# One store of a fused scan and adapter kernel, issued as 16 transfers of 8 partitions

## The chip, the core and the metric

The kernel runs on one core of a Trainium2 chip. The metric is the time of one execution on the device in microseconds (us). A measurement of this kernel repeats within about 0.2%.

## What is computed

The first part is a linear recurrence along 6400 steps for 8 sequences of 128 channels; the second adds, for each of the 51200 resulting rows, the weighted output of two of eight low-rank adapters.

```python
h = np.zeros((B, D))                       # B, S, D = 8, 6400, 128
for t in range(S):
    h = a[:, t] * h + b[:, t]
    out[:, t] = h
x = out.reshape(B * S, D)                  # 51200 x 128
topk = the two largest of x @ w_gate       # w_gate: 128 x 8
w = softmax over these two
x + sum over the two of w * ((x @ A[e]) @ B[e])   # A: 8 x 128 x 16, B: 8 x 16 x 128
```

The inputs a and b are 26.2 MB each, the output is 26.2 MB, all in float32.

## The kernel before

The 51200 rows are cut into 100 units of 512 rows (`UT`). For each unit w or v:

- `AB`: TensorE transposes a and b of the unit (64-row blocks, line 88) into `pA` and `pB`, so that the channels lie on partitions; ScalarE copies a to `a_st` (`aev`).
- `scan`: one VectorE scan instruction over 512 steps makes x in `xT`, in float16, from the last value of the unit before.
- `L`, the gating steps and `sig`: logits, the two largest, a sigmoid, in groups of units.
- `Z`, `mul`, `T`, `tev`: x times all adapters' A, times the gates, transposed back.
- `R` and `D`: x and the adapters' outputs are summed in `pO`; `oev` copies `pO` to a slot of `outt`, which holds `NOUT` = 24 units. In the last ten units (`TAIL`) VectorE may do this copy too; before that it is ScalarE's.
- `st`: a store of two units (one at either end: units 0, 1 and 96 to 99) from `outt` to the output. With two units a partition holds 1024 numbers, 4 KB, which are contiguous in the output; a store of two units is 128 such rows, 512 KB. Loads have the same shape.

Nothing is ordered by hand. `_Plan` (from line 94) takes every operation with its cost, its key (unit plus an offset by kind) and what it depends on, simulates the engines, and writes out one instruction list for each engine, with waits on semaphores in between. All loads and stores are issued by SP on one queue, in the planner's order, by `add_dma` (line 303), which gives each slot of `outt` a semaphore of its own that a transfer raises by 16. The lines concerned:

- `store(j)`, line 841: a store of units from u0 on has the key u0 + `HOLD` (24), and while u0 + 24 is under `FREE` (96) it also waits for the scan of unit u0 + 24. So stores run 24 units behind the scan, and the store of units 60 and 61 waits for the scan of unit 84. It is the first store after the last load on SP.
- `o_evac(v)`, line 819: the copy of unit v waits for the store that frees its slot, that of unit v - 24. So the copies of units 84 and 85 wait for the store of units 60 and 61.
- `ends`, line 875: SP's last instruction waits for the last 24 stores.

After the last load come 22 stores: 18 of two units and four of one.

Of the kernel before, what the change touches and what calls it, by code (L numbers as in the profile page):

```python
# [23 lines left out]
HOLD = 24  # L24
FREE = 96
# [7 lines left out]
NOUT = 24  # L33
TAIL = 10
FILLS = 1


class _Op:
# [55 lines left out]
class _Plan:  # L94
# [9 lines left out]
    def add(self, name, eng, kind, unit, cost, emit, deps=(), dma=None, bank=None, mode=None):  # L104

        engs = (eng,) if isinstance(eng, str) else eng
        cost = cost if isinstance(cost, dict) else {e: cost for e in engs}
        self.ops[name] = _Op(name, engs, kind, unit, cost, emit, list(deps), dma, bank, mode)
# [98 lines left out]
def bass_associative_scan_2x2__then__mixture_of_adapters_kernel(  # L207
# [8 lines left out]
    NB, S, D = a.shape  # L216
# [34 lines left out]
    with ExitStack() as stack:  # L251
# [20 lines left out]
        outt = sb(nc.sbuf_tensor("outt", [128, NOUT, UT], F32))  # L272
# [30 lines left out]
        def add_dma(name, eng, unit, starts, slot, time, deps=()):  # L303

            if slot not in dma_sem:
                dma_sem[slot] = [sb(nc.semaphore("q_" + "_".join(map(str, slot)))), 0]
            dma_sem[slot][1] += 16 * len(starts)
            sem, value = dma_sem[slot]

            def emit(h):  # L310
                for dst, src in starts:
                    last = h.dma_start(dst, src).then_inc(sem, 16)
                return last

            add(name, eng, "dma", unit, (450.0 * len(starts), 0.0), emit, deps, (sem, value, time))
# [54 lines left out]
        def fill(w):  # L370


            def emit(h):
                for _ in range(3):
                    last = h.matmul(pO[1][:, :], warm_t[:, 0:128], warm_t[:, :])
                return last

            add(f"fill{w}", "pe", "fix", 1000.0, (600.0, 800.0), emit, [f"AB{w}"])

        for w in range(FILLS):  # L380
            fill(w)
# [410 lines left out]
        def delta(v):  # L792
            def emit(what):
                def run(h):
                    for q, w in [(q, w) for q in range(Q) for w in what]:
                        left, right = {"x": (x_rows(v, q), ident_h[:, :]), "d": (zw_rows(v, q), Bcat_h)}[w]
                        last = h.matmul(
                            pO[v % NO][:, q * 128 : (q + 1) * 128],
                            left,
                            right,  # L800
                            start=w == "x" and q == 0,
                            stop=w == "d",
                            skip_group_check=True,
                        )
                    return last

                return run
# [7 lines left out]
            else:  # L815
                add(f"R{v}", "pe", "R", v, (223.0, 423.0), emit("x"), deps, mode="full")
                add(f"D{v}", "pe", "D", v, (220.0, 420.0), emit("d"), [f"R{v}", "cstB"] + tevs, mode="full")

        def o_evac(v):
            def emit(h):  # L820
                copy = h.tensor_copy if plan.ops[f"oev{v}"].eng == "dve" else h.copy
                return copy(outt[:, v % NOUT, :], pO[v % NO][:, :])  # L822

            tail = v >= NU - TAIL
            add(
                f"oev{v}",
                ("act", "dve") if tail else "act",
                "oev",
                v,
                {"act": (477.0, 645.0), "dve": (600.0, 745.0)} if tail else (477.0, 645.0),  # L830
                emit,
                [f"D{v}", f"st{store_of.get(v - NOUT)}"],
            )

        stores, u = [], 0
# [3 lines left out]
        store_of = {v: j for j, (u0, n) in enumerate(stores) for v in range(u0, u0 + n)}  # L839

        def store(j):
            u0, n = stores[j]
            s0 = u0 % NOUT
            rows = out[u0 * UT : (u0 + n) * UT, :].rearrange("(p i) d -> p (i d)", p=128)
            add_dma(
                f"st{j}",
                "sp",
                u0 + HOLD,
                [(rows, outt[:, s0 : s0 + n, :].rearrange("p n c -> p (n c)"))],
                ("o", s0, n),  # L850
                1.036 * ((625.0 if n == 2 else 650.0) * n + 13.0),
                [f"oev{v}" for v in range(u0, u0 + n)] + [f"scan{u0 + HOLD}"] * (u0 + HOLD < FREE),
            )

        for w in range(NU):
            for t in "ab":
# [6 lines left out]
        for v in range(NU):  # L863
            logits(v)
            z_mm(v)
            z_mul(v)
            zw_tr(v)
            t_evac(v)
            delta(v)
            o_evac(v)  # L870
        for k in range(len(groups)):
            gating(k)
        for j in range(len(stores)):
            store(j)
        ends = [f"st{j}" for j in range(len(stores) - NOUT, len(stores))]
        add("end", "sp", "fix", 1.0e9, (10.0, 10.0), lambda h: h.nop(), ends)

        plan.schedule(700.0, 3000.0, lambda t: 400.0, 94.0)
# [49 lines left out]
```

## Time and profile before

| | |
|---|---|
| median of 3 runs | 204.37 us (204.33 to 204.53) |
| the profiled execution | 204.59 us, span 202.5 us |
| TensorE / VectorE / ScalarE / GpSimd busy | 191.3 / 183.6 / 175.4 / 115.5 us |
| moved by DMA | 79.35 MB, 392 GB/s in the mean |
| TensorE's granted clock | 0.994 |

The span is that of the profiled instructions and transfers on the core; the execution's own time contains a start and an end beside it. Busy times overlap each other, so they say which engines are near their limit and not what ends last. A DMA share is the mean busy share of the core's 16 DMA engines: 1.0 is all sixteen at work, 1/16 (0.06) is one of them. "To landing" is from the issue of a transfer on SP to the last of the 16 steps by which its semaphore rises, and so tells of its slowest engine. L312 is the line of the `dma_start` call in `add_dma`.

### The profile page before, as it was taken

The numbers are of one execution on the slowest core, as the hardware profiler recorded it, in microseconds if no ns is written. First come the engines' busy times: TensorE is split into PE (matmuls) and PEld (weight loads), VectorE is DVE, ScalarE is ACT, GpSimd is POOL, SyncE is SP. The second block draws the span as 40 slices with busy tenths as digits, with TensorE's granted clock in tenths as the row PEclk, the third lists the DMA queues.
The fourth block names the chain that finished last, engine by engine and source line by source line (L and its number), as shares of the span: only waits on it lengthen the run. The fifth ranks groups of instructions, "written<-read, shape, count | busy, mean of one in ns | idle before, by whom it ended". The sixth has DMA issues, their size and how long they took to land.

```text
span 202.5 us, 8755 instructions
## 1 busy us (share of the span) xinstructions
PE 191.3 (94%) x3594; PEld 171.2 (85%) x3594; DVE 183.6 (91%) x272; ACT 175.4 (87%) x385; POOL 115.5 (57%) x234
## 2 busy tenths in 40 slices
PE   7888898999999999999999999999999999999990
PEld 3667777889899999999999999999999999999880
DVE  1599889999999999999999999999999999989960
ACT  2357977788999999999999999999999999989981
POOL 1326775766656746746665674675666575874300
PEclk9999999999999999999999999999999999999997
DMA  7999999999999999999999999999999999997875
GB/s 177 401 410 409 403 408 405 405 404 408 410 408 412 412 414 414 408 413 413 410 411 416 414 411 412 413 412 415 410 415 410 411 413 416 409 414 313 317 302 198
DMA packets 23687, 79.35 MB, mean 392 GB/s; under 512 B 3680, under 2 KB 3808, under 8 KB 23648
## 3 DMA queue, kind: packets, MB, share of 16 engines
q1 hardware_dynamic: 22320, 78.65, 97.2%
q8 instruction: 29, 0.48, 1.0%
q10 hardware_dynamic: 1328, 0.14, 0.5%
q14 instruction: 10, 0.08, 0.1%
HBM read 52.56 MB, written 26.21 MB: 389 GB/s over the span
## 4 chain that ended last, share of the span: by engine, by line
PE 83%; ACT 6%; DVE 4%; issue 3%; POOL 2%; DVEq 0%
PE pA L88 27%; PE pO L84 23%; PE pTL L88 14%; PE pZ L84 10%; PE pTL L84 5%; DVE xT L511 3%; PE pB L88 3%; ACT a_st L492 3%; PE pB L84 2%; ACT outt L822 1%; ACT zwT L787 1%; ACT z_sb L716 1%; DVE mx L590 1%; POOL zw L730 1%; ACT Lg L584 0%
## 5 line engine op out<-in xcount | busy, mean ns | idle before, releaser
L511 DVE TENSOR_TENSOR_SCAN xT<-a_st,xT,pB 128x512 f16<-128x512 f32 x96 | 120.2, 1252 | 3.8 <-ACT a_st L492 1.3
L492 ACT COPY a_st<-pA 128x512 f32<-128x512 f32 x100 | 60.7, 607 | 19.1 <-PE pB L88 14.9
L88 PE MATMUL pA<-ident_f,a_in 64*128 64x64 f32 (+1 forms) x792 | 71.8, 230 | 2.8 <-ACT a_st L492 1.9
L88 PE MATMUL pB<-ident_f,b_in 64*128 64x64 f32 (+1 forms) x792 | 71.7, 230 | 0.3 <-issue 0.2
L88 PEld LDWEIGHTS pA<-ident_f,a_in 64*128 64x128 f32 (+1 forms) x792 | 57.8, 139 | 11.3 <-ACT a_st L492 3.3
L822 ACT COPY outt<-pO 128x512 f32<-128x512 f32 x97 | 60.0, 626 | 0.7 <-PE pO L84 0.2
L787 ACT COPY zwT<-pTL 128x512 f16<-128x512 f16 x95 | 58.5, 615 | 0.4 <-PE pTL L88 0.3
L88 PEld LDWEIGHTS pB<-ident_f,b_in 64*128 64x128 f32 (+1 forms) x792 | 57.4, 138 | 1.1 <-issue 0.8
L730 DVE TENSOR_TENSOR zw<-pZ,g 128x512 f16<-128x512 f32 x76 | 51.5, 680 | 1.4 <-PE pTL L88 0.8
L84 PE MATMUL pO<-ident_h,xT 128*128 128x128 f16 x400 | 41.5, 228 | 0.2
L84 PE MATMUL pZ<-cst_h,xT 128*128 128x128 f16 x400 | 38.1, 219 | 0.0
L84 PE MATMUL pO<-cst_h,zwT 128*128 128x128 f16 x400 | 37.3, 218 | 0.8 <-ACT zwT L787 0.4
L88 PE MATMUL pTL<-ident_h,zw 128*128 128x128 f16 x380 | 37.7, 222 | 0.0
L730 POOL TENSOR_TENSOR zw<-z_sb,g 128x512 f16<-128x512 f32 x24 | 25.4, 1060 | 20.1 <-PE pTL L84 18.3
L84 PEld LDWEIGHTS pO<-ident_h,xT 128*128 128x128 f16 x400 | 32.8, 147 | 0.8 <-ACT outt L822 0.3
L84 PE MATMUL pTL<-cst_h,xT 128*128 128x8 f16 x400 | 27.5, 174 | 1.0 <-DVE xT L511 0.9
L84 PEld LDWEIGHTS pZ<-cst_h,xT 128*128 128x128 f16 x400 | 27.8, 114 | 0.1
L88 PEld LDWEIGHTS pTL<-ident_h,zw 128*128 128x128 f16 x380 | 21.6, 97 | 6.0
L84 PEld LDWEIGHTS pO<-cst_h,zwT 128*128 128x128 f16 x400 | 23.8, 97 | 1.9 <-PE pO L84 1.8
L84 PEld LDWEIGHTS pTL<-cst_h,xT 128*128 128x128 f16 x400 | 23.5, 117 | 2.0 <-DVE xT L511 1.5
L626 POOL TENSOR_TENSOR d<-Lg,m 128x128 f32<-128x128 f32 (+3 forms) x27 | 10.2, 378 | 20.8 <-DVE m L619 20.7
L661 POOL TENSOR_SCALAR pn<-d 128x128 f32<-128x128 f32 (+3 forms) x29 | 16.6, 572 | 2.5
(41 smaller groups left out, 137.9 us busy)
## 6 DMA issues: line engine op xcount, KB each, us to landing
a_in<-in_a_dram SPq DMA_DIRECT2D x49, 512.0 KB, 14.7
b_in<-in_b_dram SPq DMA_DIRECT2D x49, 512.0 KB, 14.4
out_dram<-outt SPq DMA_DIRECT2D x47, 512.0 KB, 14.6
out_dram<-outt SPq DMA_DIRECT2D x6, 256.0 KB, 3.7
a_in<-in_a_dram SPq DMA_DIRECT2D x2, 256.0 KB, 9.0
b_in<-in_b_dram SPq DMA_DIRECT2D x2, 256.0 KB, 4.3
cst_f<-in_moe_A_dram ACTq DMA_DIRECT2D x1, 64.0 KB, 3.9
cst_f<-in_moe_B_dram ACTq DMA_DIRECT2D x1, 64.0 KB, 5.2
```

The costliest lines, as they stand in the source:

```text
L84: return self.h.matmul(*args, **kw)
L88: return self.h.transpose(*args)
L492: lambda h: h.copy(a_st[w % 2][:, :], pA[0][:, :]),
L511: last = h.tensor_tensor_scan(out=x_at(lo, hi), data0=a_st[w % 2][:, lo:hi], data1=pB[w % 2][:, lo:hi], initial=init, op0=ALU.mult, op1=AL ...
L590: last = h.max(mx[s][:, j, :], Lg[s][:, j, :])
L626: lambda h: h.tensor_tensor(out=v(d1[s]), in0=v(Lg[s]), in1=bc(m1[s]), op=ALU.subtract),
L661: lambda h: h.tensor_scalar(v(pn[s]), v(d2[s]), 0.0, -1.0e30, ALU.is_lt, ALU.mult),
L716: lambda h: h.copy(src[:, :], pZ[v % NZ][:, :]),
L730: lambda h: h.tensor_tensor(out=oview, in0=zview, in1=gview, op=ALU.mult),
L787: lambda h: h.copy(*evacuated(v)),
L822: return copy(outt[:, v % NOUT, :], pO[v % NO][:, :])
```

## The change

The store of units 60 and 61 (512 KB, 128 partitions of 4 KB) is issued as 16 transfers of 8 partitions (32 KB) each, one after another at the same place in SP's order. Each has a semaphore of its own. The copies of units 84 and 85, and SP's last instruction, wait for all 16. All other stores and loads stay as they are, and so does the order of the instructions on TensorE, VectorE, ScalarE and GpSimd.

```diff
+SPLIT = (60,)
...
+        def pieces(j):
+            return [f"st{j}"] + [f"st{j}p{k}" for k in range(1, 16)]
+
         def o_evac(v):
...
-                [f"D{v}", f"st{store_of.get(v - NOUT)}"],
+                [f"D{v}"] + pieces(store_of.get(v - NOUT)),
             )
...
             rows = out[u0 * UT : (u0 + n) * UT, :].rearrange("(p i) d -> p (i d)", p=128)
-            add_dma(
-                f"st{j}",
-                "sp",
-                u0 + HOLD,
-                [(rows, outt[:, s0 : s0 + n, :].rearrange("p n c -> p (n c)"))],
-                ("o", s0, n),
-                1.036 * ((625.0 if n == 2 else 650.0) * n + 13.0),
-                [f"oev{v}" for v in range(u0, u0 + n)] + [f"scan{u0 + HOLD}"] * (u0 + HOLD < FREE),
-            )
+            slots = outt[:, s0 : s0 + n, :].rearrange("p n c -> p (n c)")
+            size = 8 if u0 in SPLIT else 128
+            for k in range(128 // size):
+                part = slice(k * size, (k + 1) * size)
+                add_dma(
+                    f"st{j}p{k}" if k else f"st{j}",
+                    "sp",
+                    u0 + HOLD,
+                    [(rows[part], slots[part])],
+                    ("o", s0, n, k) if k else ("o", s0, n),
+                    1.036 * ((625.0 if n == 2 else 650.0) * n + 13.0) * size / 128,
+                    [f"oev{v}" for v in range(u0, u0 + n)] + [f"scan{u0 + HOLD}"] * (u0 + HOLD < FREE),
+                )
...
-        ends = [f"st{j}" for j in range(len(stores) - NOUT, len(stores))]
+        ends = [x for j in range(len(stores) - NOUT, len(stores)) for x in pieces(j)]
```

## The prediction

> **What bounds the kernel now.** I read the page first, for what is busy and which chain ended last; then the last pieces of that chain; then the DMA share in windows towards the end; then single transfers, from issue to landing.
>
> ```profile
> span 202.5 us, 8755 instructions
> ...
> DMA  7999999999999999999999999999999999997875
> ...
> q1 hardware_dynamic: 22320, 78.65, 97.2%
> ...
> PE 83%; ACT 6%; DVE 4%; issue 3%; POOL 2%; DVEq 0%
> ```
> ```profile
> 197.72 0.58 ACT outt L822
> ```
>
> The chain is TensorE's for 83% of the span. It ends with ScalarE's copy at 197.72 + 0.58 = 198.3 us, 4.2 us before the span does, and what follows it is a store. Both limits stand side by side: TensorE and the transfer queue (97.2% of 16 engines' span). So the end must be read from the queue.
>
> ```profile
> 160.00:170.00 10.00, 9.72 (x22) 1.00 1.02 410
> 182.00:186.00 4.00, 4.00 (x10) 1.00 0.81 323
> 186.00:190.00 4.00, 3.88 (x11) 1.00 0.76 304
> 190.00:194.00 4.00, 3.39 (x8) 1.00 0.77 307
> 195.25:195.50 0.25, 0.15 (x2) 1.00 0.05 16
> 195.50:195.75 0.25, 0.25 (x1) 1.00 0.09 33
> 199.50:199.90 0.40, 0.00 (x0) 0.94 0.99 374
> 200.10:201.00 0.90, 0.00 (x0) 0.50 0.06 25
> 201.20:201.60 0.40, 0.00 (x0) 0.50 0.00 0
> ```
>
> These are windows: stretch, length, ScalarE's busy time, TensorE's granted clock, the DMA share (mean of 16 engines) and GB/s. Up to 170 all sixteen engines are full. From 182 on a fifth to a quarter of them is free. At 195.25 the share is 0.05 and from 200.10 to 201.00 it is 0.06: one sixteenth, so one engine works and fifteen have nothing. That last stretch in detail:
>
> ```profile
> DMA packets 12, 0.02 MB, mean 25 GB/s; under 512 B 1, under 2 KB 1, under 8 KB 12
> ...
> q1 hardware_dynamic: 12, 0.02, 6.5%
> ```
>
> 12 packets in 0.9 us one behind the other, 25 GB/s, which is what one of sixteen engines moves at 410 GB/s (25.6). A single engine is still clearing a backlog when the other fifteen are done. Its landings say since when:
>
> ```profile
> L312 SPq DMA_DIRECT2D out_dram<-outt x1: 1150/1150/1150, 160.3 to 160.3; - x1
> ...
> DMA to landing us min/median/max: 15.4/15.4/15.4
> ```
> ```profile
> L312 SPq DMA_DIRECT2D out_dram<-outt x4: 332/332/333, 196.0 to 198.3; - x4
> ...
> DMA to landing us min/median/max: 3.3/3.5/3.7
> ```
> ```profile
> 160.26 38.40 SPq L312 DMA_DIRECT2D out_dram<-outt  x22
> ```
>
> A transfer has landed when its slowest engine has. The store of units 60 and 61 is issued at 160.26 and lands at 160.26 + 15.4 = 175.7; the last of 22 stores lands at 198.3 + 3.3 = 201.6. The last four stores are half the size, so behind the first one stand 17 + 2 = 19 full stores in 25.9 us: 1.365 us each. The whole queue in the window 160 to 170 needs 0.524 MB / 410 GB/s = 1.28 us for one. So the lone engine is slower than the rest by 0.085 us a store (1.365 - 1.28), it arrives at 160 already late, and it works without a gap to the end. What bounds the end is this one engine's backlog of rows, by about 1.1 us over the other fifteen (200.0 against 201.1, when data ends; landing follows 0.5 us later, at 201.6).
>
> **The change, part by part.**
>
> *Rows to engines.* How a store of 128 rows is dealt out shows in the counts of the stretch 160.2 to 182:
>
> ```profile
> DMA packets 2522, 8.98 MB, mean 412 GB/s; under 512 B 277, under 2 KB 277, under 8 KB 2517
> ```
>
> Eight large packets to each small one (2240 to 277): an engine gets 8 rows of a store and one small packet that tells of the end. So the 512 KB store puts 8 rows on every engine, the slow one too. A piece has 8 rows in all. If a row isn't cut, a piece occupies at most eight engines with one row each. If these are the same eight each time, they get 16 rows in place of 8, and the other eight get none. The change then moves 256 KB from one half of the engines to the other.
>
> For an engine that gets more: 8 rows at 0.160 us (4096 B at 25.6 GB/s) = +1.28 us, +1.37 us for the slow one (8 x 1.365 / 8). For an engine that is spared: -1.28, the slow one -1.37. The fifteen small packets more: the last four stores have twice as many small packets for their bytes and land 0.63 us apart (199.7 to 201.6, three steps), which isn't over half of 1.365; so nothing to about 0.05 us each, 0 to 0.8 us in all, and I take 0, the nearest row.
>
> The Trainium skill, "DMA: Bandwidth & Descriptors", section "Why a DMA increments its semaphore by 16 and not by 1", says that a transfer from this queue uses the largest number of engines up to 16 that divides the outermost dimension, and always the lowest-numbered. By that a piece runs on eight, the same each time; no transfer of before is that small, so no row shows it.
>
> *Where the slow engine is spared* (the case I take). Its data ends at 201.1 - 1.37 = 199.7. Then the other fifteen are last. Now they end at about 200.0 (share 0.99 up to 199.90, 0.06 from 200.10), held by the last issue at 198.33. Do eight of them, with 1.28 us more, end later? They idle 19 to 24% of 182 to 194, some 2.6 us each in the mean; but all but one have caught up by 195.25 for certain (0.05), so the worst of them may have done so only there. It would then end at 195.25 + 1.28 + 1.28 (store issued at 195.0) + 4 x 0.64 = 200.4. So data ends between 200.0 and 200.4, and the gain is 0.7 to 1.1 us. Most engines idle long before 195, so I take the upper end: 1.1.
>
> *Issue on SP.* One issue becomes 16.
>
> ```profile
> 0.74 0.38 SPq L312 DMA_DIRECT2D a_in<-in_a_dram  x1
> 1.17 0.42 SPq L312 DMA_DIRECT2D b_in<-in_b_dram  x1
> 1.64 0.42 SPq L312 DMA_DIRECT2D a_in<-in_a_dram  x1
> ```
> ```profile
> 159.09 1.07 SPq L312 DMA_DIRECT2D a_in<-in_a_dram  x1
> 160.26 1.15 SPq L312 DMA_DIRECT2D out_dram<-outt  x1
> ```
> ```profile
> L312 SPq DMA_DIRECT2D a_in<-in_a_dram x1: 1075/1075/1075, 159.1 to 159.1; - x1
> ...
> DMA to landing us min/median/max: 15.1/15.1/15.1
> ```
>
> Where there is room in the queue an issue takes 0.38 to 0.42 us and the next follows 0.05 later; where the queue is full, 1.07 to 1.15. The store at 160.26 meets a full queue, so the first piece takes 1.15 and is done at 161.4. The other fifteen bring one sixteenth of the bytes each, so I take 0.45: 15 x 0.45 = 6.8 us, SP free at 168.2. Queued behind on SP are the 21 later stores alone; every load is issued before (159.09 is the last one) and stays ahead in the queue. The cover is the backlog: that load lands at 159.09 + 15.1 = 174.2, so up to there the slow engine has work without any store. The few stores that have been held up by then go out at some 0.4 us each, by about 170. An engine that is ahead of the slow one may run dry for a us or two; it idles later anyway. Cost: 0.
>
> *Waits.* The copy of unit 84 into the same slots must wait for 16 counters in place of one; in the built program ScalarE gets eight wait instructions of two counters each where one stood, and SP some eight more at the very end. SP's rows price one: 0.10 between 159.09 + 1.07 and 160.26, with a wait instruction in between, against 0.05 without. Seven more are 0.35 us.
>
> ```profile
> 181.73 0.60 ACT L787 COPY zwT<-pTL 128x512 f16<-128x512 f16 x1
> 182.20 0.62 ACT L822 COPY outt<-pO 128x512 f32<-128x512 f32 x1
> ```
>
> The copy at 182.20 is unit 84's; the one before it runs 0.60 us, during which the sequencer can do 0.35 us of waits. I cost it at 0. Without that cover it is 0.35 us on an engine that is busy 4.00 of 4.00 us in 182 to 186, and up to that much later at the end. The counters themselves stand by 177 to 178 (175.7 plus 1.3 for the second set of rows), 4 us before. SP's extra waits, 8 x 0.05, fall between its last issue (198.7) and the last landing. No other engine's order changes.
>
> *Sum.* 0 (issue) + 0 (waits) - 1.1 (end of data): span 202.5 to 201.4. The profiled execution took 204.59 us, 2.1 outside the span, and 0.22 over the median of 204.37. From the median: 204.37 - 1.1 = **203.3 us**.
>
> **The rivals.**
>
> *The slow engine is among the eight that get more.* Nothing is spared: its data ends 1.37 us later, 204.37 + 1.37 = **205.7 us**, up to 205.9 with some price for small packets. It decides by place alone: the same mechanism with the other sign. Against it stands only a lean of mine: one lone laggard is likelier to be the last in the order in which rows are dealt out than one of the first eight. No row numbers the engines, so I put it no higher than about 7 to 3.
>
> The Trainium skill, same page, "Latency and other measured facts", names engines 7 and 15 as usually slower: one in each half. The windows at 195.25 and 200.10 show one slow engine, not two, so that rule doesn't decide it.
>
> *The pieces are spread evenly*, by cutting rows or by other engines for each piece: the slow engine keeps its share, the change does nothing that it seems to, **204.4 us**.
>
> *The pieces are held one by one.* If the queue takes a number of transfers rather than of rows, each piece waits as full-size ones do: 15 x 1.2 = 18 us, SP free at 179.4. The slow engine is out of loads when its last one ends, at about 173.7, and idles until 180.1 (a store reaches its engines some 0.7 us after issue: issued at 195.03, the share is 0.09 up to 195.75), then needs 25.9 us: landing at 206.5, **209 us**. It begins to cost from (173.0 - 161.4) / 15 = 0.77 us a piece. For it: 1.07 and 1.15 in a full queue. Against it: sixteen pieces hold one store's rows.
>
> The Trainium skill, same page, section "Rules for kernel authors", says that transfers under 64 KB pay mostly overhead; a piece has 32 KB. If each held the queue as long as a full store does, that would be an estimated 15 x 1.28 = 19 us more, this rival's size. The issues at 0.74, 1.17 and 1.64 overlap freely, but those are of 256 KB and more: no row shows a 32 KB one.
>
> **How the numbers follow.** Slow engine spared 0.57; slow engine loaded 0.27; spread evenly, or a gain eaten by waits, 0.09; held one by one 0.07. About 0.2% (0.4 us) is what a measurement of this kernel can tell from no change. So faster 0.57, same 0.09, slower 0.34. The likeliest case alone has 203.1 to 203.9 (0.35 of waits and the later catching up included). The range takes in the rival with the other sign and its price: 203.0 to 205.9. Left out are the held pieces and the odd ends, 0.1 to 0.15.
>
> **What would show it.** Right: sixteen issues from 160.26 at 0.4 to 0.5 us; no window of share 0.06 behind the last full one; last store landing about 2.2 us after issue; unit 84's copy at 182.2. Wrong: a lone engine that works 1.4 us longer (loaded); the same 1 us tail (spread); issues above 0.77 us and a fall of the share before 182 (held).

## The result, and the profile after

The changed kernel takes 206.21 us (206.08 to 206.28, median of 3 runs) where the kernel before takes 204.37: a ratio of 1.0087, with an interval of 1.0064 to 1.0110. It is slower by 1.84 us. The forecast was 203.3 with a range of 203.0 to 205.9.

The page of the changed kernel; its profiled execution took 206.08 us:

```profile
span 204.3 us, 8785 instructions
...
PE 191.4 (94%) x3594; PEld 171.3 (84%) x3594; DVE 183.6 (90%) x272; ACT 175.5 (86%) x385; POOL 115.5 (57%) x234
...
DMA  7999999999999999999999999999999999998682
...
q1 hardware_dynamic: 22432, 78.65, 96.6%
...
q14 instruction: 11, 0.09, 0.1%
```

The engines are as busy as before (TensorE 191.4 us against 191.3). The queue moves the same bytes in 112 more packets (22432 against 22320). If each of 16 pieces ends with one small packet on each of its engines, and the whole store did so on 16, then 16 x n - 16 = 112, and n is 8: a piece runs on eight engines.

The windows of the changed kernel, read as those of the prediction (stretch, length, ScalarE busy, granted clock, DMA share, GB/s):

```profile
160.00:170.00 10.00, 9.72 (x23) 1.00 1.02 406
182.00:186.00 4.00, 4.00 (x10) 1.00 0.87 349
186.00:190.00 4.00, 3.88 (x9) 1.00 0.80 319
190.00:194.00 4.00, 3.39 (x9) 1.00 0.71 281
195.75:196.00 0.25, 0.25 (x1) 1.00 0.05 16
199.50:199.90 0.40, 0.00 (x0) 1.00 1.05 394
200.10:201.00 0.90, 0.00 (x0) 1.00 0.23 87
201.00:202.00 1.00, 0.00 (x0) 1.00 0.05 14
202.00:203.00 1.00, 0.00 (x0) 0.83 0.06 25
203.00:204.00 1.00, 0.00 (x0) 0.50 0.02 8
```

The lone window between two stores is still there (share 0.05, now at 195.75), and the lone stretch at the end is longer: before, one engine worked from 200.1 to 201.1; now it works until after 203. A lone engine that works longer is the sign that the prediction names for a slow engine that gets more rows. From 201 to 202 it moves only 14 GB/s, where a lone engine moved 25 before; that has a cause of its own, below.

Where the time came in is seen at the next store, that of units 62 and 63. Its issue and time to landing, first before, then after:

```profile
L312 SPq DMA_DIRECT2D out_dram<-outt x1: 1008/1008/1008, 161.5 to 161.5; - x1
...
DMA to landing us min/median/max: 15.6/15.6/15.6
```
```profile
L313 SPq DMA_DIRECT2D out_dram<-outt x1: 361/361/361, 167.3 to 167.3; - x1
...
DMA to landing us min/median/max: 11.5/11.5/11.5
```

It landed at 161.5 + 15.6 = 177.1 and now lands at 167.3 + 11.5 = 178.8. By the times of the semaphore steps, which are finer, 177.07 and 178.85: 1.79 later. The last load had already landed 0.23 later (174.45 against 174.22), before any piece, so the pieces put 1.56 us on the slow engine. Eight rows more at 1.365 / 8 are 1.37; 0.19 is left, which I put down to the small packets (by the 0.18 us a row of runs 2 and 9, below, it would be 0.12). The steps show the same directly: a piece's semaphore rises by steps of eight engines, and the last of them, the slow engine's, come at 174.64, 174.83 and so on to 177.66, every 0.20 us: sixteen rows, one in each piece.

The issues and waits delay nothing that the end waits for, as forecast. SP's rows of the changed kernel, and ScalarE's two copies there:

```profile
L313 SPq DMA_DIRECT2D out_dram<-outt x16: 295/301/1258, 160.4 to 166.9; - x16
```
```profile
182.04 0.60 ACT L788 COPY zwT<-pTL 128x512 f16<-128x512 f16 x1
182.51 0.62 ACT L826 COPY outt<-pO 128x512 f32<-128x512 f32 x1
```

The first piece took 1.26 us, the second 0.68, the others some 0.30. SP is free at 167.2. Unit 84's copy starts 0.3 later than before, by no more than the shift that stands at 156 us already, ahead of the pieces.

The end, by the last four stores:

```profile
L313 SPq DMA_DIRECT2D out_dram<-outt x4: 332/332/333, 196.3 to 198.6; - x4
...
DMA to landing us min/median/max: 5.1/5.2/5.5
```

The last issue is 0.3 later than before and the last landing 2.15 (203.75 against 201.60, by the semaphore steps). Of these 2.15, 0.23 stood there ahead of the pieces and 1.56 are the pieces. The other 0.36 came in behind the store of units 62 and 63, where an instruction fetch falls. The DMA view of the changed kernel in a stretch of 0.3 us from 200.9 shows it starting:

```profile
DMA packets 1, 0.01 MB, mean 27 GB/s; under 512 B 0, under 2 KB 0, under 8 KB 0
...
q14 instruction: 1, 0.01, 6.4%
```

One packet of 8 KB took 0.31 us on the engine that is already last, and the packets after it were slower for a while (0.13 to 0.22 us each where 0.08 was usual): from 200.91 to 201.71 that engine got through three rows, which take 0.24 us otherwise, so 0.56 was lost. That is more than 0.36. Run 2, which has no fetch ahead of its end, is 0.26 us faster than before over this same stretch, so a deeper backlog wins some time back; why isn't shown. Before, the fetch at the end came behind the last landing. SP runs more instructions now, issues and waits, and its program reaches the next piece of code while the slow engine still works. From the last landing to the end of the profiled execution it was 2.99 us before (204.59 - 201.60) and is 2.33 now (206.08 - 203.75), so part of what the fetch costs comes back there.

### The profile page after: what moved, and what is told of

It is laid out like the page before. It is cut to its first block, busy times and chain, and to the rows that moved or that the text cites. A ratio compares the mean times of both kernels' runs of the same rounds, so it can differ in the third digit from the quotient of the medians.

```text
span 204.3 us, 8785 instructions
## 1 busy us (share of the span) xinstructions
PE 191.4 (94%) x3594; PEld 171.3 (84%) x3594; DVE 183.6 (90%) x272; ACT 175.5 (86%) x385; POOL 115.5 (57%) x234
## 3 DMA queue, kind: packets, MB, share of 16 engines
q1 hardware_dynamic: 22432, 78.65, 96.6%
## 4 chain that ended last, share of the span: by engine, by line
PE 78%; ACT 8%; DVE 4%; DMA 3%; issue 3%; SPq 1%; POOL 1%; DVEq 0%; ACTq 0%
PE pA L89 25%; PE pO L85 22%; PE pTL L89 13%; PE pZ L85 10%; PE pTL L85 5%; ACT a_st L493 3%; DVE xT L512 3%; DMA b_in<-in_b_dram 3%; PE pB L89 3%; ACT outt L826 2%; ACT zwT L788 1%; ACT z_sb L717 1%; SPq L313 1%; DVE mx L591 0%; ACT Lg L585 0%
```

## The experiments

All of them change only how the store of units 60 and 61 is cut, unless it is said otherwise. `SPLIT` becomes a table with (first partition, partitions, column part, column parts) for each transfer. Each transfer has a semaphore of its own, as in the change. Times are medians beside runs of the kernel before on the same chip.

**1. Sixteen transfers that load all engines alike.**

```diff
-SPLIT = (60,)
+SPLIT = {60: [(16 * k, 16, c, 2) for k in range(8) for c in range(2)]}
```

> The store of units 60 and 61 goes out as 16 transfers as in the changed kernel, but each of 16 partitions and half a row (2 KB), so that every one of the 16 engines gets one half row of each: as many transfers, issues, semaphores and waits as the change has, without moving bytes from one engine to another. Theory 'place' (the slow engine is one of the eight that the 8-partition pieces use, and carries 16 rows in place of 8): the slow engine's bytes are unchanged; 16 small packets at some 0.03 us (16 rows with theirs took 3.2 us in the changed kernel, against 16 x 0.171) are 0.5 us, and the instruction fetch that the changed kernel shows behind 200.9 us may add 0.5: 204.8 to 205.4 us. Rival 'pieces' (the price is that of 16 small transfers, wherever they run): 206.2 us, as the changed kernel.

Measured: 205.33 us (205.32 to 205.54), ratio 1.0048, 1.0034 to 1.0061. The last four stores of this kernel:

```profile
L313 SPq DMA_DIRECT2D out_dram<-outt x4: 332/332/333, 195.9 to 198.2; - x4
...
DMA to landing us min/median/max: 4.6/4.8/5.2
```

As many issues and waits as in the change, and half of the loss. So the number of transfers alone doesn't make the whole of it. This half is a cost of its own: a single row of 2 KB per engine and transfer took the fast engines 0.17 us by the semaphore steps, against 0.16 for a row of 4 KB inside a whole store. With its rows cut in half, this run alone doesn't show that the place makes the rest; runs 2, 6 and 9 change the place without small pieces. The store behind landed 0.8 us later than before, net of the shift ahead of it.

**2. Two transfers, with seven engines loaded.** 119 partitions are 7 x 17, 9 are left.

```diff
+SPLIT = {60: [(0, 119, 0, 1), (119, 9, 0, 1)]}
```

> The store of units 60 and 61 goes out as two transfers, of 119 and of 9 partitions. 119 is 7 x 17 and has no larger divisor up to 16, so by the rule of the Trainium skill it runs on the first seven engines, 17 rows each; 9 partitions run on the first nine, one row each. Theory 'place', if the slow engine is the eighth: it carries 1 row in place of 8, ends 1.2 us earlier, and the last store's other engines are last: 203.2 to 203.5 us, faster than both kernels. If the slow engine is one of the first seven: 18 rows in place of 8, 1.7 us more: 206.1 us. Rival 'pieces': two transfers in place of one cost next to nothing: 204.4 us.

Measured: 205.98 us (205.70 to 206.03), ratio 1.0072, 1.0058 to 1.0086. Its last four stores:

```profile
L313 SPq DMA_DIRECT2D out_dram<-outt x4: 332/332/332, 196.4 to 198.7; - x4
...
DMA to landing us min/median/max: 4.7/4.9/5.1
```

The case in which the slow engine is the eighth fell: it is one of the first seven. The rival that many small transfers are what costs fell too: two transfers cost nearly as much as sixteen, with 17 + 1 rows on the slow engine in place of 8. The store behind lands 1.80 us later, net of the shift ahead of it: 0.18 for each of the ten rows more. The last landing is 1.77 later.

The Trainium skill, "DMA: Bandwidth & Descriptors", section "Why a DMA increments its semaphore by 16 and not by 1", says that the number of engines is the largest up to 16 that divides the outermost dimension on both sides of the transfer, and that they are the lowest-numbered. The traces agree with the number: by the steps of the semaphores 8 partitions ran on 8 engines, 119 on 7, 9 on 9. None of them numbers the engines; "first" and "fifth" here mean the order in which transfers of growing size take them.

**3. More instructions on SP, the store left whole.**

```diff
+SPLIT = {}
...
+        for i in range(23):
+            add(f"idle{i}", "sp", "fix", 84.0, (10.0, 10.0), lambda h: h.nop().then_inc(s_idle, 1), ["scan84"])
```

> The store is whole, as before; SP gets 23 instructions more at its place that only raise an unused semaphore, so that SP has as many instructions as in the changed kernel. In the changed kernel an 8 KB instruction fetch runs at 200.9 us on the engine that is last, in the kernel before at 202.8 us, behind the end. Theory 'fetch comes earlier': 23 more instructions bring SP to its next page before the end, the fetch meets the slow engine's backlog: 0.3 to 0.6 us more, 204.7 to 205.0 us, and the fetch is seen before the last landing. Rival (SP's instructions cost nothing, the end's extra time is all the pieces'): 204.4 us, no fetch before the end.

Measured: 204.69 us (204.40 to 204.81, 11 runs), ratio 1.0010, 1.0001 to 1.0019. The DMA view from 190 to 203, and the last four stores:

```profile
q14 instruction: 1, 0.01, 0.2%
```
```profile
L313 SPq DMA_DIRECT2D out_dram<-outt x4: 332/332/332, 196.5 to 198.8; - x4
...
DMA to landing us min/median/max: 3.3/3.5/3.7
```

The fetch moved ahead of the end, to 194.5, and the last landing moved by 0.48 us. The time rose by 0.2 alone, less than I expected: the rest came back between the last landing and the end, which was 2.51 us here against 2.99. So about 0.2 us of the loss belongs to SP's program being longer. The interval reaches from nothing to 0.4.

**4. The same pieces on one semaphore.** ScalarE's wait instructions are as before.

```diff
-                    ("o", s0, n, k) if k else ("o", s0, n),
+                    ("o", s0, n),
```

> The change as it is, with one semaphore for all 16 pieces: ScalarE's copy of unit 84 and SP's end wait for one counter, as before. ScalarE has the instructions of before, SP 7 fewer than the changed kernel (221 in place of 228; 205 before). Theory 'place': the slow engine's 16 rows stay, +1.6 us: 206.0 us, or 206.2 if the fetch still falls before the end; the waits were free. Rival 'waits' (the eight wait instructions before unit 84's copy delay the last stores): the end comes 0.3 us earlier and the last issue with it, 205.9 us, with the fetch as in the changed kernel.

Measured: 206.01 us (205.91 to 206.22), ratio 1.0075, 1.0061 to 1.0089. Unit 84's copy and the last four stores:

```profile
182.87 0.62 ACT L826 COPY outt<-pO 128x512 f32<-128x512 f32 x1
```
```profile
L313 SPq DMA_DIRECT2D out_dram<-outt x4: 332/332/332, 196.7 to 199.0; - x4
...
DMA to landing us min/median/max: 4.6/4.7/5.2
```

The times that I expected with and without a price for the waits (205.9 and 206.2, with the fetch as in the change) lie too close together for this measurement. The trace tells more: the copy isn't earlier than the change's (182.87 against 182.51), and neither is the last issue (199.0 against 198.6). So the waits held nothing up.

**5. Finding the engine.** The store in transfers of 112, 1, 2, 3, 4 and 6 partitions, so that each of the last five reaches a little further into the order of the engines.

```diff
+SPLIT = {60: [(0, 112, 0, 1), (112, 1, 0, 1), (113, 2, 0, 1), (115, 3, 0, 1), (118, 4, 0, 1), (122, 6, 0, 1)]}
```

> The store of units 60 and 61 goes out as six transfers of 112, 1, 2, 3, 4 and 6 partitions, in this order. If a transfer of n of the small ones runs on the first n engines, its landing is that of the slowest among these. The slow engine is 6.5 us behind the fastest at this place, and 174 to 176 us is where it works on this store; the others are up to 6.2 us behind. Theory 'place': the landing jumps to over 175 us at the first transfer that includes the slow engine and stays there; if even that of 6 does not, the slow engine is the seventh. If the slow engine were not tied to a place in this order (rival: whichever engine is last at the time), the landings would rise bit by bit with no jump to the slow engine's landing. The time is not read from this run: the slow engine gets 8 to 12 rows.

Measured: 204.45 us in one run, against 204.24 for the kernel before. What counts are the last steps of the six semaphores, in us:

```
partitions     112       1       2       3       4       6
last step   175.60  169.02  171.84  172.01  172.25  175.79
```

The transfer on all engines lands at 175.60, which is the slow engine's time. Those on one to four engines land over 3 us sooner; that on six lands with the slow engine. So on this chip it is the fifth or the sixth. The chip of this run and of runs 6 to 8 is another one than that of runs 1 to 4.

**6. Sparing it.** 116 partitions are 4 x 29: four engines get 29 rows, and the other 12 partitions put one row on each of twelve engines. The slow one gets 1 row in place of 8.

```diff
+SPLIT = {60: [(0, 116, 0, 1), (116, 12, 0, 1)]}
```

> The store of units 60 and 61 goes out as two transfers, of 116 partitions (4 x 29: on the first four engines, 29 rows each) and of 12 (one row on each of the first twelve). In the locating run a transfer of 4 landed at 172.3 us and one of 6 at 175.8, so the slow engine is the fifth or sixth. Theory 'place': it carries 1 row in place of 8 and ends 1.2 us earlier; the first four engines get 22 rows more, 3.5 us, which they catch up before 195; then the last issue sets the end, and the last landing is about 200.5 in place of 201.6 us: 203.2 to 203.5 us, faster than both kernels by 0.5%. Rival (any unequal dealing costs, since some engine is overloaded): 205 us or more, with a lone engine at work behind 200.5 us.

Measured: **203.59 us** (203.34 to 203.94), ratio 0.9961, 0.9948 to 0.9974: faster than both kernels, and just above the 203.2 to 203.5 that I expected. Its last four stores, and two of its windows:

```profile
L313 SPq DMA_DIRECT2D out_dram<-outt x4: 332/332/332, 196.5 to 198.8; - x4
...
DMA to landing us min/median/max: 2.1/2.2/2.4
```
```profile
200.10:201.00 0.90, 0.00 (x0) 0.82 0.35 130
201.00:201.60 0.60, 0.00 (x0) 0.50 0.00 0
```

The last store lands 2.1 us after its issue, and the share at the end is 0.35 and then 0: sixteen engines stop together, and no lone stretch is left. Even the four engines with 22 rows more each (29 + 1 in place of 8) had caught up. That is the mechanism which the prediction forecast, with the place the other way about.

**7. Sixteen small transfers that spare it.** 64 partitions, then 16 pieces of four partitions, which run on the first four engines.

```diff
+SPLIT = {60: [(0, 64, 0, 1)] + [(64 + 4 * k, 4, 0, 1) for k in range(16)]}
```

> The changed kernel's form with another width: half of the store as one transfer of 64 partitions (4 rows on every engine), the other half as 16 transfers of 4 partitions each, which run on the first four engines. Theory 'place': 16 small transfers again, but none on the slow engine, which carries 4 rows in place of 8: it ends 0.7 us earlier; the instruction fetch of SP may take back 0.2 to 0.5: 203.7 to 204.2 us. Rival 'pieces' (small transfers cost wherever they run): 205.3 to 206.2 us.

Measured: 204.08 us (203.98 to 204.38, 11 runs), ratio 0.9988, 0.9979 to 0.9997. Its seventeen issues, and the last four stores:

```profile
L313 SPq DMA_DIRECT2D out_dram<-outt x17: 268/295/1197, 160.2 to 167.8; - x17
```
```profile
L313 SPq DMA_DIRECT2D out_dram<-outt x4: 332/332/333, 196.7 to 199.0; - x4
...
DMA to landing us min/median/max: 2.6/2.7/3.0
```

With pieces half as large as the change's and one transfer more, the kernel is a little faster than before (0.1%, with an interval that ends just below 1). Four rows fewer on the slow engine outweigh the issues, the waits and a fetch at 198.8. Between pieces of 8 and pieces of 4 the sign turns, and with it the rows on one engine: 16 there, 4 here, 8 in the whole store. (Here half of the store stays whole, and the chip is another, so this run shows the sign and not the size.)

**8. Sparing it wholly.** 124 partitions are 4 x 31; the last 4 run on four engines too.

```diff
+SPLIT = {60: [(0, 124, 0, 1), (124, 4, 0, 1)]}
```

> Two transfers, of 124 (4 x 31) and of 4 partitions: the first four engines carry 32 rows each, the other twelve none. Theory 'place': the slow engine ends 1.4 us earlier, but the last issue sets the end, as with one row on it: 203.2 to 203.5 us. If the first four are then late themselves (24 rows more, 3.8 us): up to 204.0 us.

Measured: 203.55 us (203.18 to 203.99), ratio 0.9962, 0.9950 to 0.9974, the same as run 6. The last store lands 2.1 us after its issue here too. With 1 row or none on the slow engine the end is the same: what holds it is now the last issue, and no other dealing of this store helps past that.

**9. Five engines.** 115 partitions are 5 x 23.

```diff
+SPLIT = {60: [(0, 115, 0, 1), (115, 13, 0, 1)]}
```

> Two transfers, of 115 partitions (5 x 23: the first five engines, 23 rows each) and of 13 (one row on each of the first thirteen). If the slow engine is the sixth, it has 1 row in place of 8 as with 116 and 12: 203.5 us. If it is the fifth, it has 24 rows, 16 more at 0.171: its backlog ends 2.7 us later, 206.9 to 207.2 us. A rival by which small numbers of engines are good in themselves gives 203.5 us either way, so only the slow result would add to theory 'place'.

Measured: 206.76 us (206.70 to 207.06), ratio 1.0111, 1.0094 to 1.0128. The last four stores, and the windows at the end:

```profile
L313 SPq DMA_DIRECT2D out_dram<-outt x4: 332/332/333, 196.2 to 198.6; - x4
...
DMA to landing us min/median/max: 5.6/5.8/6.0
```
```profile
201.00:202.00 1.00, 0.00 (x0) 1.00 0.06 23
202.00:203.00 1.00, 0.00 (x0) 0.72 0.06 25
203.00:204.00 1.00, 0.00 (x0) 0.50 0.05 18
```

This run was on the chip of runs 1 to 4. So there the slow engine is one of the first five; on the chip of runs 5 to 8 the first four spare it, and it is the fifth or the sixth. If both chips have it at the same place, it is the fifth; no run tests that on one chip alone. Sixteen rows more moved the store behind by 2.85 us net of the shift ahead of it, 0.18 a row as in run 2, and the last landing by 2.53 (204.13), 0.158 a row. I had reckoned with 0.171 and the time is just under what I expected.

**10. Two stores in pieces of 8.**

```diff
+SPLIT = {u: [(8 * k, 8, 0, 1) for k in range(16)] for u in (60, 62)}
```

> The change made to two stores, those of units 60, 61 and of units 62, 63: 32 pieces of 8 partitions. Theory 'place': the slow engine gets 16 rows more than before in place of 8: its backlog grows by another 1.4 us for the rows and 0.2 for their small packets: 206.2 + 1.6 = 207.8 us. If the extra time of the change were paid once (SP's fetch, a wait, the first piece's full queue): 206.2 to 206.6 us.

Measured: 207.39 us (207.38 to 207.56), ratio 1.0142, 1.0125 to 1.0159. The last four stores:

```profile
L313 SPq DMA_DIRECT2D out_dram<-outt x4: 332/332/333, 196.7 to 199.0; - x4
...
DMA to landing us min/median/max: 6.0/6.2/6.5
```

A second store in pieces costs another 1.2 us over the change's 206.21 (1.3 on the last landing). It adds up store by store, as rows on one engine do; a cost that is paid once would have left it at 206.2 to 206.6. It is less than the 1.6 that I expected. Net of how late the last load already was (0.23 in the change, 0.09 here) the second store adds 1.4 us on the last landing, near the first one's 1.56; the runs don't tell the rest.

## Why the prediction was wrong

**What bounds the end: right.** One engine's backlog did. Sparing it took the lone stretch away (run 6), loading it made that longer (the change, runs 2, 9 and 10).

**Rows to engines: right.** Eight engines to a piece, the same eight each time; they get 16 rows and the others none.

**"Where the slow engine is spared (the case I take)": this step failed.** I had no row that numbers the engines and put the slow one late in the order by a lean of "7 to 3". It is one of the first six of sixteen on either chip (run 9, run 5), and in the changed kernel each piece ends with its step, from 174.64 to 177.66: it was among the eight that get more, and the store behind landed 1.56 us later in place of earlier. The first rival, "by place alone: the same mechanism with the other sign", is what happened. The lean rested on nothing that a profile of the kernel before shows. With the evidence at hand the two places were equally likely, and a forecast that said so would have put the two cases side by side.

**The terms of that rival: two too small.** It gave 205.7, "up to 205.9 with some price for small packets".
- The 1.37 us for eight rows held nearly: runs 2 and 9 have 0.18 a row, 1.4 for eight, and the store behind landed 1.56 later in all.
- The small packets, taken at 0 from a range of 0 to 0.8, are put at the other 0.19. No run changes them alone.
- Not in the sum: SP's longer program brings an instruction fetch onto the slow engine ahead of the end. With the store left whole, 23 more instructions on SP cost 0.2 us (run 3). I looked at what the extra instructions take on SP, and not at their code having to be fetched through the same engines.

1.37 + 0.19 + 0.2 = 1.76, against 1.84 measured: by these two terms 206.21 lies above 205.9.

**Issue on SP: right, and cheaper than forecast.** Pieces took 0.30 us where I reckoned 0.45, and the rival in which they are held one by one didn't come.

**Waits: right.** With one semaphore in place of sixteen nothing came earlier (run 4).

**The gain if it were spared: nearly right.** The prediction gave 0.7 to 1.1 us and took the upper end. Run 6, which spares the engine by another dealing, measured 0.81, and the last store landed 2.1 us after its issue, where 2.2 was named as the sign. The floor was the last issue, as the prediction had it.

## What to carry to other kernels

Where the DMA share at the end of a kernel falls to one sixteenth, one engine is late, and cutting a transfer anew helps or hurts by which engines get its rows. Find the late engine's place first, with a few small transfers of 1, 2, 3 and more partitions in one run, before reasoning about which half it is in; then choose the partition counts so that engines with time to spare take its share (here 116 + 12). Count also the instructions that are added on the issuing engine, since their code is fetched through the same DMA engines (here 8 KB, 0.31 us on the engine that was late).

## What the hardware showed that I had not expected

- One engine is slower than the rest on both chips that were tried, among the first five in order on one and the fifth or sixth on the other, and it falls behind on stores. In the trace of before, from the first to the last semaphore step of successive transfers (issued from 133 to 146 us) it is, in us:

```
store  load  load  store  load  load  store  load  load  store
 5.29  5.30  5.31   5.48  5.52  5.51   5.66  5.70  5.75   5.87
```

  It grows by 0.12 to 0.17 with a store and by 0.05 or less with a load. The Trainium skill, "DMA: Bandwidth & Descriptors", section "Latency and other measured facts", says that engines 7 and 15 are usually slower; here it was a single engine, one of the first six in order, that set the end. Why it is slow on stores stays open.
- An engine works through its share of a store on its own: transfers on the first four engines landed over 3 us ahead of the transfer that was issued before them (run 5).
- A transfer's only row on an engine hardly gets cheaper when it is cut in half: by the steps a fast engine took 0.17 us for each 2 KB in run 1 and 0.19 for each 4 KB in the change. Inside a larger transfer it does: the last four stores of before have rows of 2 KB and land 0.62 to 0.65 us apart, 0.08 for each of eight rows, against 0.16 for 4 KB.
- One instruction fetch of 8 KB took an engine 0.31 us and slowed the three packets behind it.
